# Taking GpSimd out of a second phase's weight conversions, and queueing the attention's conversions later

## The chip, the cores and the metric

One core of a Trainium2 chip runs the whole program. The metric is the device time of one execution in microseconds (us). The engines are TensorE (PE: matrix multiply; PEld: its weight loads), VectorE (DVE), ScalarE (ACT), GpSimd (POOL) and SyncE (SP), which here issues all the DMAs.

## The reference

Causal attention over 4 batches of 8 heads (576 tokens, head size 64) with a bias from a running sum, then two feed-forward blocks on 2304 tokens, all in float32:

```python
scores = scale * np.matmul(q, k.transpose(0, 1, 3, 2))
...
attn = np.exp(scores)                      # after the row maximum is taken off
attn = attn / (np.sum(attn, axis=-1, keepdims=True) + 1e-09)
x = np.matmul(attn, v)                     # -> (2304, 512)
a = x @ w1                                 # (512, 1024)
b = x @ w2
h = a * b @ w3
x2 = h @ w_out                             # (1024, 512)
h = x2 @ w_in                              # (512, 1024)
sm = softmax(h)
solu = h * sm
ln = (solu - mean) / sqrt(var + 1e-06) * g_ln
out = ln @ wo2                             # (1024, 512)
```

## The kernel before

Every large product is done as three products of split operands: a value is held as a high part (`...H`, written by a copy that rounds, `hi`) and a low part (`...L`, the value less its high part, `lo`), and PE adds high by high, high by low and low by high. The weights arrive as 64-bit floats in two 32-bit words, in jobs of 512 KB (a tile `stage` of 128 rows by 512 values), and are converted on the chip. One job is `to_f32` (a scaling of the upper words by a power of two, then three DVE instructions on lines 376, 377 and 380 that shift and join the words), then `hi` on ACT and `lo`. Two things of a job are placed on an engine by a table: the scaling (line 370 on ACT, line 372 on POOL) and the `lo` (line 97, on DVE or POOL). `ME = [(None, G), (G, V)]` deals this out in the second phase in turn: one job is scaled on ACT and its `lo` is on POOL, the next is scaled on POOL and its `lo` is on DVE. The last weight, wo2, has its own conversion, with both on POOL. A `stage` buffer is free for the next load when its `lo` has read it; there are two such buffers in the attention and four after it.

The program runs in stages that overlap a little.
- Attention, 32 heads in steps: PE makes scores (`sc`), DVE takes the maximum with line 203, ACT the exponential with line 207, DVE and ACT normalise, PE transposes (`tr`) and multiplies by v (`av`). `late` holds the `av` products of a pair of heads until the next step. Conversions of w1 and w2 (16 jobs, `wab_job`, always scaled on ACT with `lo` on DVE) are put in by `pump` in steps 3 to 17, and from step 10 the products `a` and `b` of the first block (`ab_unit`, pieces of 12 matmuls) are laid between the attention's steps as `fill`.
- The last `ab` units, with the conversions of w_out and w3 pumped between them (32 jobs with those of w_in, which `w_job` places).
- `m_unit`: the product M of w3 and w_out in 8 blocks f of 24 matmuls; each block is evicted as MH[f] by ACT and ML[f] by DVE.
- `x2_unit(c, m)`: for 256 tokens c and a column block m of 128 it adds 24 matmuls over k = 0 to 7 with MH and ML. The last k needs the last block of M. The first c has its columns done one at a time (`XMS`).
- The loop over 18 token tiles t: `h_unit` (48 matmuls in two halves of 24 and 512 columns, then the chain maximum, exponential, product, square, power on POOL, scaling with line 706), `tr2` (transposes of the result), `out_unit` (24 matmuls with wo2).

Program order alone does not set the order on an engine. A scheduler runs a model of the engines when the program is built and writes each engine's queue; `tc.issue_after(x)` holds what is issued in its scope behind x. On the chip each queue runs in order: an instruction that waits holds all that stand behind it on its engine.

Of the kernel before, what the change touches and what calls it, by code (L numbers as in the profile page):

```python
# [25 lines left out]
def tile_attention_moe(  # L26
# [15 lines left out]
    nc = tc.nc  # L42
# [38 lines left out]
    def bigtile(name):  # L81
        return PSP[0].tile([128, 2, 512], F32, tag="A", name=name)

    def smalltile(name):
        return PSP[1].tile([128, 512], F32, tag="B", name=name)
# [10 lines left out]
    def lo(dst, src, hi_, eng=nc.vector):  # L96
        eng.tensor_tensor(out=dst, in0=src, in1=hi_.bitcast(F32), op=ALU.subtract)  # L97
# [17 lines left out]
    STAT = [at.tile([128, 16], F32, name=f"STAT{i}") for i in range(PB)]  # L115

    after = [None]
    raw_t = {}
    VT = [at.tile([128, 5, 2, D], F32, name=f"VT{i}") for i in range(2)]
    XHE = None  # L120
# [71 lines left out]
    def softmax_tile(h, ti, ps_in, cut=None):  # L192
        q0, rows, n, o = QT[ti]
        pt = p_t[h]
        st = STAT[h % PB]
        dst = pt[0:rows, o:o + n]
        msk = wmask[0:rows, S - n:S] if rows == 128 else wmask[0:rows, S - 128:S - 64]
        if cut:
            dst2 = dst.rearrange("p (a b) -> p a b", a=cut)
            msk = msk.rearrange("p (a b) -> p a b", a=cut)  # L200
        else:
            dst2 = dst
        nc.vector.tensor_tensor_reduce(  # L203
            out=dst2, in0=ps_in, in1=msk, scale=-SCALE, scalar=BIG,
            op0=ALU.add, op1=ALU.min, accum_out=st[0:rows, ti:ti + 1],
        )
        nc.scalar.activation(  # L207
            out=dst, in_=dst, func=AF.Exp, bias=st[0:rows, ti:ti + 1], scale=-1.0,
            accum_out=st[0:rows, 5 + ti:6 + ti],
        )  # L210

    def qk_part(h, part):
        if part == 0:
# [34 lines left out]
    def tr_part(h, part):  # L248
        pt = p_t[h]
        PT_ = PT[h % 4]  # L250
        ps = smalltile("tr")

        def evict(dst, src):
            cnt[0] += 1
            hi(dst(PT_), src, PCOPY[cnt[0] % len(PCOPY)])

        def blk(j, q0, q1):
            o = KO[j] - 128 * j
            return lambda t: t[:, o + q0:o + q1]

        ev = []
        if part == 0:
            full = [(0, i, (i - 1) * 128) for i in range(1, 5)]
            ev = [(0, 512, blk(0, 64, S))]
        elif part == 1:
            full = [(1, i, (i - 2) * 128) for i in range(2, 5)] + [(3, 4, 384)]
            ev = [(0, 384, blk(1, 192, S)), (384, 512, blk(3, 448, S))]
        elif part == 2:
            full = [(2, i, (i - 3) * 128) for i in range(3, 5)]
            ev = [(0, 256, blk(2, 320, S))]  # L270
        else:
            full = []
        for j, i, c in full:
            nc.tensor.transpose(ps[:, c:c + 128], pt[:, QOF[i] + 128 * j:QOF[i] + 128 * j + 128], ident)  # L274
        if part == 2:
            nc.tensor.transpose(ps[0:64, 256:320], pt[0:64, QOF[0]:QOF[0] + 64], ident[0:64, 0:64])
        for c0, c1, d in ev:
            evict(d, ps[:, c0:c1])
        if part == 2:
            evict(lambda t: t[0:64, 0:64], ps[0:64, 256:320])  # L280
        if part == 3:
            for i in range(1, 5):
                nc.tensor.transpose(
                    ps[0:64, 64 * i:64 * i + 64],
                    pt[64:128, QOF[i] + 128 * i:QOF[i] + 128 * i + 64],
                    ident[64:128, 64:128],
                )
            for j in (1, 3):
                src = ps[0:64, 64 * j:64 * j + 128].rearrange("p (a b) -> p a b", a=2)
                evict(lambda t: half_view(t, j), src)  # L290
            p_t.pop(h)

    cnt = [0]
    PCOPY = [None, V]

# [94 lines left out]
        lo(dst_l, t, dst_h, e2)  # L390

    V, G = nc.vector, nc.gpsimd
    ME = [(None, G), (G, V)]
    MAT = ()
    WO2 = (0, 4, 0, 0, 0, 2, 2)
    XMS = ((0,), (1,), (2,), (3,))
    EX = 0
    AP3, AM = (2, 2, 2, 2, 2, 2, 1, 1), (3, 3, 3, 3, 3, 3, 3, 3)
    mjobs = []
# [22 lines left out]
    def pump(n):  # L422
        for _ in range(n):
            load_jobs()
            if loaded:
                raw, conv = loaded.pop(0)
                conv(raw)
        load_jobs()

    def w_job(src, dst, eng=None):  # L430
# [80 lines left out]
    for st, (h, ph) in enumerate(steps):  # L511
        for _ in range(NF.get(st, 0)):
            fill.extend(ab_unit(*units.pop(0)))
        left = len(fill)
        if st == 11:
            ps_ctx.close()
            PSP[:] = [
                ps_ctx.enter_context(tc.tile_pool(name="psE", bufs=1, space=PSUM)),
                ps_ctx.enter_context(tc.tile_pool(name="psF", bufs=6, space=PSUM)),
            ]  # L520

        def F(share):
            while fill and len(fill) > left * (1 - share):
                fill.pop(0)()

        if h is not None:
            if NQ <= h + 2 < NH:
                load_head(h + 2)
            qk_part(h, 0)
        if st > 1:  # L530
            pump(PUMP.get(st, 0))
        if h is not None:
            qk_part(h, 1)
            qk_part(h, 2)
        F(FS)
        if h is not None:
            normalise(h)
        if ph is not None:
            for part in range(4):
                tr_part(ph, part)  # L540
        if late:
            for fn in late.pop():
                fn()
        if h is not None:
            if h % 2 == 1:
                load_v(h // 2)
            if h + 1 < NH:
                split_qk(h + 1)
            if h < 2 and h + 2 < NQ:
                aug_rows(QB[h], KB[h])  # L550
            if h + 2 < NH:
                if h + 2 < NQ:
                    load_head(h + 2)
                load_aug(h + 2, cumf_scr[h + 2:h + 3] if h + 2 < NQ else cum_scr[h + 2])
        F(1)
        if ph is not None and ph % 2:
            parts = av_parts(ph // 2)
            if ph < PD or st == len(steps) - 1:
                for fn in parts:
                    fn()  # L560
            else:
                late.append(parts)
    attn_ctx.close()


    NT = T // 128
# [85 lines left out]
    def x2_unit(c, *ms):  # L652
# [2 lines left out]
            x2_t[c] = [r2.tile([128, KC, 256], F32R, tag=f"x2{i}", bufs=2, name=f"x2{i}") for i in "hl"]  # L655
        XH, XL = x2_t[c]
        GH, GL = g_hl[c]
        ps = {m: smalltile("x2")[:, 0:256] for m in ms}
        for k0, k1 in ((0, KF - 1), (KF - 1, KF)):
            for m in ms:  # L660
                for k in range(k0, k1):
# [103 lines left out]
            raws[k] = stage(wo2[k * 128:k * 128 + 128])  # L765

    def wo2_conv(k):
        t = to_f32(raws.pop(k), G)
        nc.scalar.activation(out=t, in_=t, func=AF.Copy, scale=gln[:, k:k + 1])
        hi(OH[:, k], t)  # L770
        lo(OL[:, k], t, OH[:, k], nc.gpsimd)
        wo2_load(k + 4)

    nwo = [0]
# [1 line left out]
    def wo2_pump(c):  # L776
        for _ in range(c):
            wo2_conv(nwo[0])
            nwo[0] += 1
# [13 lines left out]
    for t in range(NT + 2):  # L793
# [7 lines left out]
        if t < NT and c + 1 < NCH and 2 * t + 1 >= EX:  # L801
            x2_unit(c + 1, 2 * o + 1)
        if t < 2:
            wo2_pump(WO2[5 + t])
        if 0 <= t - 2 < NT:
            out_unit(t - 2)
        if t == NT:
# [55 lines left out]
```

## Time and profile before

| | us |
|---|---|
| three runs | 787.57, 788.91, 792.77 |
| median | 788.91 |
| profiled execution | 790.51 |
| its span, first to last instruction | 788.70 |
| PE busy | 756.8 (96%) |
| DVE busy | 472.9 (60%) |
| ACT busy | 396.5 (50%) |
| POOL busy | 157.7 (20%) |

The profiled execution has 1.81 us outside its span and is 1.60 us above the median. A busy share is a mean over stages. Matmul ends are modelled, so the pitch of a row of matmuls (its time by its count) says more than their busy time. "PEclk" is the granted clock of TensorE as a share of its full 2.4 GHz; 0.50 is its lower level, 1.2 GHz.

### The profile page before, as it was taken

The numbers are of one execution on the slowest core, as the hardware profiler recorded it, in microseconds if no ns is written. First come the engines' busy times: TensorE is split into PE (matmuls) and PEld (weight loads), VectorE is DVE, ScalarE is ACT, GpSimd is POOL, SyncE is SP. The second block draws the span as 40 slices with busy tenths as digits, with TensorE's granted clock in tenths as the row PEclk, the third lists the DMA queues.
The fourth block names the chain that finished last, engine by engine and source line by source line (L and its number), as shares of the span: only waits on it lengthen the run. The fifth ranks groups of instructions, "written<-read, shape, count | busy, mean of one in ns | idle before, by whom it ended". The sixth has DMA issues, their size and how long they took to land.

```text
span 788.7 us, 13075 instructions
## 1 busy us (share of the span) xinstructions
PE 756.8 (96%) x4864; PEld 658.4 (83%) x4864; DVE 472.9 (60%) x1162; ACT 396.5 (50%) x927; POOL 157.7 (20%) x165
## 2 busy tenths in 40 slices
PE   8988998999999999999899979899999999999997
PEld 5556888988888898999888868788888888888886
DVE  5898889787656564328867998744424343432241
ACT  4986787698666665414325345633323243322232
POOL 6022313234222211003412546300000000000000
PEclk9998999999999999999999979999999999999999
DMA  5643454334333320016649455102022000000001
GB/s 138 197 115 102 144 172 142 104 98 131 107 92 90 94 77 31 31 63 227 209 140 345 170 183 165 54 14 68 14 67 63 31 14 14 14 15 14 14 27 40
DMA packets 38039, 75.59 MB, mean 96 GB/s; under 512 B 6796, under 2 KB 18060, under 8 KB 37976
## 3 DMA queue, kind: packets, MB, share of 16 engines
q1 hardware_dynamic: 37976, 74.76, 30.9%
q8 instruction: 38, 0.62, 0.3%
q14 instruction: 25, 0.20, 0.1%
HBM read 60.36 MB, written 14.38 MB: 95 GB/s over the span
## 4 chain that ended last, share of the span: by engine, by line
PE 75%; DVE 6%; DMA 3%; POOL 2%; issue 2%; ACT 2%; SPq 0%; ACTq 0%; DVEq 0%; POOLq 0%
PE o L732 13%; PE a L334 12%; PE b L334 11%; PE h L683 11%; PE x L663 11%; PE av L306 4%; PE tr L274 3%; PE sc L189 3%; PE sc L190 2%; PE m L589 2%; PE tr L721 2%; DMA stage<-in_w_dram 2%; DVE stage L377 1%; DVE stage L376 1%; DVE stage L380 1%
## 5 line engine op out<-in xcount | busy, mean ns | idle before, releaser
L207 ACT ACTIVATE P<-P,STAT 128x448 f32<-128x448 f32 (+4 forms) x160 | 87.9, 551 | 30.0 <-DVE STAT L203 28.6
L691 DVE TENSOR_REDUCE sv<-h 128x1 f32<-128x1024 f32 x18 | 22.0, 1223 | 114.3 <-PE h L683 114.3
L663 PE MATMUL x<-gh,MH 128*128 128x256 f32 x288 | 84.0, 292 | 3.1 <-ACT MH L92 3.1
L663 PE MATMUL x<-gh,ML 128*128 128x256 f32 x288 | 82.6, 287 | 2.2 <-DVE ML L97 2.2
L663 PE MATMUL x<-gl,MH 128*128 128x256 f32 x288 | 82.6, 287 | 0.0
L97 POOL TENSOR_TENSOR QA<-qk,QB 64x576 fp32r<-64x576 f32 x24 | 34.6, 1441 | 208.9 <-ACT QB L92 170.1
L203 DVE CUSTOM_DVE_ANT_0 P<-sc,wmask 128x448 f32<-128x448 f32 (+4 forms) x160 | 70.2, 478 | 9.5 <-PE sc L181 6.5
L705 POOL TENSOR_TENSOR sv<-sv,mhalf 128x1 f32<-128x1 f32 x18 | 10.0, 555 | 261.7 <-DVE sv L702 261.7
L334 PE MATMUL a<-xT0h,W 128*128 128x288 f32 x256 | 59.1, 305 | 2.5 <-ACT a_sb L346 1.8
L663 PEld LDWEIGHTS x<-gh,MH 128*128 128x128 f32 x288 | 56.4, 196 | 4.4 <-ACT MH L92 3.6
L334 PE MATMUL b<-xT1h,W 128*128 128x288 f32 x256 | 57.0, 297 | 2.9 <-DVE g_sb L354 2.8
L663 PEld LDWEIGHTS x<-gh,ML 128*128 128x128 f32 x288 | 56.4, 196 | 2.5 <-DVE ML L97 2.4
L334 PE MATMUL b<-xT0h,W 128*128 128x288 f32 x256 | 58.2, 302 | 0.2 <-DVE g_sb L354 0.2
L334 PE MATMUL a<-xT1h,W 128*128 128x288 f32 x256 | 57.2, 298 | 0.5 <-ACT a_sb L346 0.5
L732 PE MATMUL o<-OH,lh 128*128 128x512 f32 x144 | 57.2, 397 | 0.3 <-ACT lh L92 0.3
L683 PE MATMUL h<-IH,x2l 128*128 128x512 f32 x144 | 56.7, 394 | 0.8 <-DVE x2l L97 0.8
L732 PE MATMUL o<-OH,ll 128*128 128x512 f32 x144 | 57.1, 396 | 0.0
L663 PEld LDWEIGHTS x<-gl,MH 128*128 128x128 f32 x288 | 56.4, 196 | 0.8
L732 PE MATMUL o<-OL,lh 128*128 128x512 f32 x144 | 56.9, 395 | 0.0
L683 PE MATMUL h<-IL,x2h 128*128 128x512 f32 x144 | 56.5, 392 | 0.0
L683 PE MATMUL h<-IH,x2h 128*128 128x512 f32 x144 | 56.2, 390 | 0.0
L693 ACT ACTIVATE e<-h,sv 128x1024 f32<-128x1024 f32 x18 | 20.1, 1115 | 66.7 <-DVE sv L691 66.7
(125 smaller groups left out, 1995.5 us busy)
## 6 DMA issues: line engine op xcount, KB each, us to landing
stage<-in_w_dram SPq DMA_DIRECT2D x32, 512.0 KB
qk<-in_qk_dram SPq DMA_DIRECT2D x48, 288.0 KB
g_scr<-g_sb SPq DMA_DIRECT2D x32, 288.0 KB
stage<-in_wo_dram SPq DMA_DIRECT2D x16, 512.0 KB
graw<-g_scr SPq DMA_DIRECT2D x6, 1024.0 KB
out_dram<-o SPq DMA_DIRECT2D x18, 256.0 KB
VT<-in_vm_dram SPq DMA_DIRECT2D x16, 256.0 KB
stage<-in_w_in_dram SPq DMA_DIRECT2D x8, 512.0 KB
```

Of the source, the lines that this page charges most:

```text
L97: eng.tensor_tensor(out=dst, in0=src, in1=hi_.bitcast(F32), op=ALU.subtract)
L189: nc.tensor.matmul(view, QB[h % 2][:, q0:q0 + rows], KB[h % 2][:, c0:c0 + w], start=True, stop=False)
L203: nc.vector.tensor_tensor_reduce(out=dst2, in0=ps_in, in1=msk, scale=-SCALE, scalar=BIG, op0=ALU.add, op1=ALU.min, accum_out=st[0:rows, ti ...
L207: nc.scalar.activation(out=dst, in_=dst, func=AF.Exp, bias=st[0:rows, ti:ti + 1], scale=-1.0, accum_out=st[0:rows, 5 + ti:6 + ti],)
L274: nc.tensor.transpose(ps[:, c:c + 128], pt[:, QOF[i] + 128 * j:QOF[i] + 128 * j + 128], ident)
L306: nc.tensor.matmul(st["ps"][64 * e:64 * e + 64, 448 + c0:448 + c1], vr[:, j, e], PT[(2 * p + e) % 4][:, o + c0:o + c1], **kw,)
L334: nc.tensor.matmul(ps, w_[:, c, fs], x_[:, c, sl], start=(c == 0 and w_ is WH and x_ is XH), stop=(c == KC - 1 and w_ is WL),)
L663: nc.tensor.matmul(ps[m], w_[:, k, m * 128:m * 128 + 128], g_[:, k], start=(k == 0 and w_ is MH and g_ is GH), stop=(k == KF - 1 and w_ is ...
L683: nc.tensor.matmul(ps[:, hf], x_[:, k, ts_], w_[:, k, hf * 512:hf * 512 + 512], start=(k == 0 and x_ is XH and w_ is IH), stop=(k == KC - ...
L691: nc.vector.reduce_max(out=sv[:, 0:1], in_=psf, axis=AX.X, negate=True)
L693: nc.scalar.activation(out=e, in_=psf, func=AF.Exp, bias=sv[:, 0:1], scale=1.0, accum_out=sv[:, 1:2])
L732: nc.tensor.matmul(ps, l_[:, k], w_[:, k], start=(k == 0 and l_ is LH and w_ is OH), stop=(k == KF - 1 and l_ is LL),)
```

## The change

In the second phase every conversion has its scaling on ACT and its `lo` on DVE (`ME` has one entry), and so has wo2. The first `x2_unit` takes all four columns in one call: first k = 0 to 6 of all four, then the last k of each; two of the four sums lie in a large PSUM tile that otherwise holds `h`. The conversions of wo2 that stood in the loop over t at entries 5 and 6 of `WO2` are at 2 and 3, with the same counts. In the attention, a pumped conversion is held behind the first maximum and the first exponential of its step (`behind`, set in `softmax_tile`), and the held `av` products behind the last transposition (`last_tr`).

```diff
-        nc.vector.tensor_tensor_reduce(
+        mx = nc.vector.tensor_tensor_reduce(
...
-        nc.scalar.activation(
+        ex = nc.scalar.activation(
...
+        if ti == 0:
+            behind[:] = [mx.ins, ex.ins]
...
-                nc.tensor.transpose(
+                last_tr[0] = nc.tensor.transpose(
...
-    ME = [(None, G), (G, V)]
+    ME = [(None, V)]
...
-    WO2 = (0, 4, 0, 0, 0, 2, 2)
-    XMS = ((0,), (1,), (2,), (3,))
+    WO2 = (0, 4, 2, 2)
+    XMS = ((0, 1, 2, 3),)
...
                 raw, conv = loaded.pop(0)
-                conv(raw)
+
+                with ExitStack() as order:
+                    for ins in behind:
+                        order.enter_context(tc.issue_after(ins))
+                    conv(raw)
...
-            for fn in late.pop():
-                fn()
+            with tc.issue_after(last_tr[0].ins):
+                for fn in late.pop():
+                    fn()
...
-        ps = {m: smalltile("x2")[:, 0:256] for m in ms}
+        if len(ms) == KC:
+            two = bigtile("x2")
+            ps = {m: smalltile("x2")[:, 0:256] if m < 2 else two[:, m - 2, 0:256] for m in ms}
+        else:
+            ps = {m: smalltile("x2")[:, 0:256] for m in ms}
...
-        t = to_f32(raws.pop(k), G)
+        t = to_f32(raws.pop(k), None)
...
-        lo(OL[:, k], t, OH[:, k], nc.gpsimd)
+        lo(OL[:, k], t, OH[:, k])
```

Each line after the first of these edits stands four or more lines lower in the changed kernel (line 203 becomes 204, 370 becomes 374, 376, 377 and 380 become 380, 381 and 384).

The first place is ACT's queue in the attention, in the softmax of head 7 (`STAT_102`), before the change:

```order
L240 ACTIVATE P<-P,STAT_101 128x448
L92 ACTIVATE W_105<-stage 128x4x128
L207 ACTIVATE P,STAT_102<-P,STAT_102 128x448
L370 ACTIVATE stage<-stage 128x512
L207 ACTIVATE P,STAT_102<-P,STAT_102 64x64
L92 ACTIVATE KA<-qk_606 128x576
```

and the same place in the changed kernel:

```order
L243 ACTIVATE P<-P,STAT_101 128x448
L92 ACTIVATE PT_95<-tr 64x2x64
L208 ACTIVATE P,STAT_102<-P,STAT_102 128x448
L208 ACTIVATE P,STAT_102<-P,STAT_102 64x64
L92 ACTIVATE KA<-qk_606 128x576
```

The scaling of a job (line 370) stood between two exponentials of the head and is gone from there: ACT's next one now follows the first exponential of head 8.

The second place is ACT's queue at the evictions of M's last two blocks (`MH<-m`), with the conversions of w_in (`IH`), before:

```order
L370 ACTIVATE stage<-stage 128x512
L92 ACTIVATE IH<-stage 128x512 x3
L92 ACTIVATE MH<-m 128x512
L370 ACTIVATE stage<-stage 128x512
L92 ACTIVATE IH<-stage 128x512
L370 ACTIVATE stage<-stage 128x512
L92 ACTIVATE IH<-stage 128x512
L92 ACTIVATE MH<-m 128x512
```

and after:

```order
L92 ACTIVATE IH<-stage 128x512
L92 ACTIVATE MH<-m 128x512
L92 ACTIVATE IH<-stage 128x512
L374 ACTIVATE stage<-stage 128x512 x2
L92 ACTIVATE IH<-stage 128x512
L92 ACTIVATE MH<-m 128x512
```

Five high parts of w_in stand ahead of the last MH before, four after; two scalings stand between the last two MH both times.

The third place is PE's queue in the attention at the first `b` piece of block f = 4 (weights `W_111` high and `W_112` low), before, where the piece runs through:

```order
L334 MATMUL b<-xT0h,W_111 128x288
L334 MATMUL b<-xT0l,W_111 128x288
L334 MATMUL b<-xT0h,W_112 128x288
L334 MATMUL b<-xT0h,W_111 128x288
L334 MATMUL b<-xT0l,W_111 128x288
```

and after, where scores of two heads stand ahead of it and a third set, of another head, behind its second matmul:

```order
L190 MATMUL sc<-KB_89,QB_87 128x288
L191 MATMUL sc<-KA,QA 128x288
L338 MATMUL b<-xT0h,W_111 128x288
L338 MATMUL b<-xT0l,W_111 128x288
L190 MATMUL sc<-KB_90,QB_88 128x448
L191 MATMUL sc<-KA,QA 128x448
L190 MATMUL sc<-KB_90,QB_88 64x64
L191 MATMUL sc<-KA,QA 64x64
```

The third matmul of the piece, the first that reads the low part, has moved behind those scores, a whole `a` piece, two more matmuls of the next `b` piece and three transpositions.

## Rows read from the trace of the kernel before

**Rows 1.** Windows by stage: span us, then each engine's busy us, PE's clock, DMA, GB/s.

```profile
16.00:140.00 124.00, 111.67 (x710) 88.38 (x710) 106.81 (x313) 98.21 (x257) 27.31 (x16) 0.94 0.51 151
140.00:355.00 215.00, 215.00 (x1689) 193.45 (x1689) 122.88 (x407) 136.36 (x367) 46.64 (x32) 1.00 0.29 82
355.00:408.90 53.90, 49.94 (x365) 48.32 (x363) 44.96 (x73) 19.71 (x38) 17.43 (x15) 1.00 0.60 198
408.90:452.57 43.67, 43.65 (x192) 36.16 (x193) 33.15 (x50) 18.65 (x32) 15.83 (x12) 1.00 0.72 239
452.57:514.00 61.43, 52.61 (x331) 48.33 (x330) 53.90 (x89) 31.77 (x58) 28.23 (x23) 0.89 0.41 135
```

**Rows 2.** Timeline of PE, 450 to 500: start, us, and in brackets the wait ahead.

```profile
457.45 0.58 PE L663 MATMUL x<-gh,ML 128*128 128x256 f32 x1 [2.15 <-DVE ML L97]
...
462.23 0.58 PE L663 MATMUL x<-gh,MH 128*128 128x256 f32 x1 [3.13 <-ACT MH L92]
...
472.97 0.40 PE L683 MATMUL h<-IH,x2h 128*128 128x512 f32 x1
...
478.45 0.50 PE L683 MATMUL h<-IH,x2l 128*128 128x512 f32 x1 [0.80 <-DVE x2l L97]
...
497.29 1.09 PE L721 MATMUL tr<-ident,so 128*128 128x128 f32 x8 [2.74 <-DVE so L706]
```

**Rows 3.** Windows behind the longest of these waits, columns as in rows 1.

```profile
457.40:467.50 10.10, 6.92 (x30) 6.63 (x31) 8.89 (x14) 3.35 (x7) 4.90 (x5) 0.50 0.54 176
...
497.20:502.00 4.80, 4.71 (x28) 4.71 (x29) 4.09 (x9) 3.60 (x7) 1.51 (x2) 0.64 0.01 3
```

**Rows 4.** Chain of waits, 511 to 526: start, us, what.

```profile
511.06 2.82 PE x L663 x24
...
519.47 5.49 PE h L683 x24
```

**Rows 5.** Groups of instructions, 355 to 500: busy us, mean ns, idle before.

```profile
L377 DVE SCALAR_TENSOR_TENSOR stage<-stage 128x512 uint32<-128x512 uint32 x40 | 33.8, 847 | 3.6 <-POOL stage L372 2.9 <-ACT stage L370 0.3
L380 DVE SCALAR_TENSOR_TENSOR stage<-stage 128x512 uint32<-128x512 uint32 x40 | 32.7, 820 | 0.2
L376 DVE TENSOR_SCALAR stage<-stage 128x512 uint32<-128x512 uint32 x40 | 23.7, 591 | 8.2 <-DMA stage<-in_wo_dram 4.1 <-DMA stage<-in_w_dram 3.4 <-DMA stage<-in_w_in_dram 0.7
L372 POOL TENSOR_SCALAR stage<-stage 128x512 f32<-128x512 f32 x24 | 21.7, 902 | 100.9 <-ACT a_sb L346 59.7 <-DMA stage<-in_w_dram 21.9 <-DMA stage<-in_wo_dram 4.4
L97 POOL TENSOR_TENSOR w3l<-stage,w3h 128x512 fp32r<-128x512 f32 x8 | 14.1, 1768 | 19.0 <-ACT w3h L92 19.0
...
L370 ACT ACTIVATE stage<-stage 128x512 f32<-128x512 f32 x16 | 11.0, 689 | 23.9 <-DMA stage<-in_w_in_dram 9.0 <-DMA stage<-in_wo_dram 8.2 <-DMA stage<-in_w_dram 6.7
...
L97 DVE TENSOR_TENSOR w3l<-stage,w3h 128x512 fp32r<-128x512 f32 x8 | 5.5, 685 | 4.4 <-ACT w3h L92 4.4
```

**Rows 6.** Instructions on the tile stage, 355 to 500: shortest, median, longest ns.

```profile
L376 DVE TENSOR_SCALAR stage<-stage x40: 414/422/1547, 356.5 to 493.9; 128x512 uint32<-128x512 uint32 x40
L377 DVE SCALAR_TENSOR_TENSOR stage<-stage x40: 673/681/1807, 357.3 to 494.9; 128x512 uint32<-128x512 uint32 x40
L380 DVE SCALAR_TENSOR_TENSOR stage<-stage x40: 672/682/1726, 358.0 to 498.3; 128x512 uint32<-128x512 uint32 x40
```

**Rows 7.** Chain of waits, 452 to 482, columns as in rows 4.

```profile
454.33 1.58 POOL IL L97
...
455.93 4.43 DMA stage<-in_w_in_dram
```

**Rows 8.** Timeline of PE, the longest of four waits between 384 and 398.

```profile
384.23 0.40 PE L334 MATMUL b<-xT1h,W 128*128 128x288 f32 x1 [1.56 <-DVE g_sb L354]
```

**Rows 9.** Timelines of PE and ACT and a window in the attention, 55 to 70.

```profile
60.22 0.41 PE L283 MATMUL tr<-ident,P 64*64 64x64 f32 x4 [1.44 <-DVE STAT L203]
...
57.54 0.67 ACT L370 ACTIVATE stage<-stage 128x512 f32<-128x512 f32 x1 [2.12 <-DMA stage<-in_w_dram]
...
60.00:70.00 10.00, 8.51 (x42) 5.17 (x42) 7.31 (x20) 5.17 (x14) 0.74 (x1) 0.66 0.54 166
```

More of the change, by code (lines that the diff above doesn't have):

```diff
@@ L117, in tile_attention_moe @@
     after = [None]
+    behind = []
     raw_t = {}
@@ L291, in tr_part @@
             p_t.pop(h)
+    last_tr = [None]
     cnt = [0]
@@ L563, in tile_attention_moe @@
     attn_ctx.close()
+    behind.clear()
     NT = T // 128
@@ L803, in tile_attention_moe @@
         if t < 2:
-            wo2_pump(WO2[5 + t])
+            wo2_pump(WO2[2 + t])
         if 0 <= t - 2 < NT:
```

## The prediction

> **What bounds the kernel now.** I first read the windows by stage, to see where PE is not the limit. Between 140 and 355 us PE is busy for all of the 215.00 us and the granted clock is 1.00 [rows 1]; nothing can be won there. The loop over token tiles behind 514 us is the same: its blocks of 24 matmuls take 2.82 and 5.49 us in an unbroken chain of PE [rows 4], and the order of its instructions is not touched. What is left lies in four places [rows 1]: the attention's first 124 us (12.3 us idle, clock 0.94, so 124 × 0.06 = 7.4 us lost to the lower level of 1.2 GHz), the tail of the `ab` units from 355 to 408.9 (4.0 us idle, clock 1.00), the blocks of M from 408.9 to 452.57 (no idle time) and the first `x2` and `h` from 452.57 to 514 (8.8 us idle, clock 0.89, 6.8 us lost).
>
> PE's timeline then says for what it waits in the last of these: 2.15 us for an ML at 457.45, 3.13 us for an MH at 462.23, 0.80 us for the low part of x2 and 2.74 us for `so` of the first token tile [rows 2]. After these pauses the granted clock is 0.50 for 10.1 us and 0.64 for 4.8 us [rows 3], so a pause costs its length and a slow stretch behind it. The attention has the same picture in small: a wait of 1.44 us at 60.22 (and one like it of 1.27 us at 62.49) and a clock of 0.66 over 60 to 70, which alone is 3.4 us [rows 9].
>
> Last I read the groups of DVE and POOL in the second phase, because the waits of M's blocks and of the tail lead to DVE. From 355 to 514 DVE is busy for 45.0 + 33.2 + 53.9 = 132 of 159 us [rows 1], so it has 27 us left. Its three shift-and-join instructions last much longer on average than in the median: 591 against 422, 847 against 681, 820 against 682 ns, with longest ones of 1547 to 1807 ns [rows 5, 6]. At 40 of each that is 6.8 + 6.6 + 5.5 = 18.9 us above the median.
>
> **The change part by part.** *POOL's share goes to ACT and DVE.* 24 scalings leave POOL (902 ns each) and cost ACT 24 × 0.689 = 16.5 us; 24 `lo` leave POOL (1768 ns each for w3) and cost DVE 24 × 0.685 = 16.4 us [rows 5]. The long instances lie where POOL works, with the `lo` on POOL itself 1.58 us long [rows 7], so with POOL quiet I expect the three DVE instructions at their medians. DVE then pays 16.4 and gets back up to 18.9 us: as a load it is between −2.5 (all of the excess gone) and +16.4 us (none), and I take about zero, since medians so close to the shortest (422 to 414, 681 to 673, 682 to 672) leave little else that could stretch the longest. The Trainium skill, "SBUF — State Buffer", section "Who interferes with whom", says that DVE and GpSimd share one pair of ports as an exclusive lock, which whoever starts first holds for its whole instruction, and that a DVE instruction with two SBUF inputs collides with GpSimd's reads; the longest of 1547 against a median of 422 agrees, and by that rule the whole 18.9 goes. ACT is busy for 45% of its time in these three windows (70.1 of 159 us) [rows 1], and 16.5 us more are covered by its idle time; the cover ends where its waits grow, which is the second rival.
>
> *The first x2.* From 452.57 to the first `h` at 472.97 the first `x2` takes 20.4 us [rows 2], where four columns at 2.82 us [rows 4] are 11.3; so 9.1 us are lost, 5.3 in the two waits [rows 2] and the rest at half clock [rows 3]. With all columns at once, 4 × 21 = 84 matmuls of 0.1175 us (2.82 by 24) stand ahead of the first that needs block 7: 9.9 us instead of 2.5. Even if MH7 comes as late as before, at about 462.2, it is then needed only at 462.4, so the 3.13 us go. The 2.15 us for ML of block 6 remain at worst: its matmul stands as early as before, and only an earlier DVE helps. The second place in the order helps a little (four instead of five high parts of w_in ahead of MH7). So the ends are −3.1 (ML6 as late as before, the half clock behind it kept) and −9.1; I take −8, because DVE on its medians should reach ML6 at least 2 us sooner: with the excess falling at 18.9 by 40 jobs, 0.47 us a job, the ten or so jobs of the M stage alone give 4.7 us, and take back about five `lo` of 0.685 = 3.4, and the tail before has done the same.
>
> *h and the norm of the first tile.* The 0.80 us for x2l should nearly stay, as two evictions at the end of four columns come in a row; the fourth column's last trio sits behind an eviction of its tile-mate. The 2.74 us for `so` and the 1.7 us of slow clock behind it (4.8 × 0.36) [rows 2, 3] stay too: line 706 of the first tile stands behind the second tile's maximum in the queue. Taken together 0, with ends of −5.2 (all of it gone) and +3 (an eviction more per pair, and a slow stretch of the length shown). wo2's conversions lie in the loop, in DVE's and ACT's idle time.
>
> *The tail.* Four waits sum to 3.2 us, the longest 1.56 us on DVE behind a queue of conversions [rows 8]. A DVE without long instances removes most: −2. The ends are −3.2 and +4: every scaling now waits on ACT for its load, and an `a_sb` eviction stands behind it.
>
> *The attention.* In the first place of the order the scaling between two exponentials of head 7 goes; it waited 2.12 us for its load there at 57.54 and held ACT's queue, and PE's two waits at 60.22 and 62.49 come right behind it [rows 9]. Gone with the slow clock, that is 1.44 + 1.27 + 3.4 = 6.1 us; since part of the slow stretch began before these waits, I take −4. Moved past are ACT's and DVE's instructions of the step and, with the release of the buffer, the next load on SP's queue. The price stands in the third place: the low part of f = 4 comes so late that its `b` piece is split, and W arrives in one burst between heads 8 and 16. DVE has some 10 us of work between the two low parts there against 6.2 us of PE's, so a wait of up to 3.8 us could appear; for the three blocks f = 4 to 6 I take +1. Together −3, ends −9 (the other two pauses of this stage vanish as well) and +6 (two such waits, less the gain).
>
> The sum: 790.5 − 8 + 0 − 2 − 3 = 777.5 us against the profiled execution, 1.81 us outside the span unchanged. That execution is 1.6 us above the median of the three runs, so 775.9, **776 us** for the median.
>
> **The rivals.** *DVE takes the place of the shared lock.* If the long instances don't come from POOL, DVE gains the 24 `lo` and loses nothing. 16 of them (8 of w_in, 8 of wo2) come behind 408.9: 11 us on an engine that is idle for 10.5 + 7.5 us there [rows 1]. ML6 and ML7 come later, x2 wins nothing, the tail neither; 790.5 − 3 − 1.6 = **786 us**. For it speaks DVE's 88% in the last window; against it the gap of mean and median in rows 6. The Trainium skill, "Perfetto Trace Analysis", section "Optimizing Scalar/DVE Operations", says that a saturated DVE may be relieved by Scalar or even GpSimd, which speaks against this change, but adds that between DVE and GpSimd it may not help.
>
> *ACT's queue becomes the bound (the slower side).* 16 scalings waited 23.9 us for loads on ACT, 1.49 us each [rows 5]; each wait holds MH, `a_sb` and high parts behind it. With 40 scalings at that wait ACT is taken for 70.1 + 16.5 + 59.8 = 146 of 159 us. It decides from 1.8 us a scaling ((159 − 86.6) / 40). A load takes 4.43 us from its buffer's release [rows 7], and the one in the attention waited 2.12 us [rows 9]: at that, ACT needs 86.6 + 84.8 = 171 us, 12 more than the stretch has, and the gains of x2 and tail are gone: 790.5 − 3 + 12 − 1.6 = **798 us**. For it speaks that POOL waited out loads for scalings till now (26.3 us); against it that POOL's slow scaling and `lo` were part of the ring that releases buffers, and that is now shorter.
>
> *More than forecast.* All pauses of the attention go (−9), ML6 is in time (−9.1), the `so` wait goes in part: 790.5 − 9 − 9.1 − 2 − 4 − 1.6 = **765 us**.
>
> *It doesn't do what it says.* The scheduler could have kept the old order; the queues show that it did not, so this has next to no chance (789 us).
>
> **How the numbers follow.** The forecast with its neighbourhood (769 to 782) has 0.60, the DVE rival 0.20, the ACT rival 0.10, the larger gain 0.08, no effect 0.02. The range reaches from 766 to 788: it takes in the DVE rival and most of the larger gain, and leaves the ACT rival out. One per cent, 7.9 us, is about what a measurement of this kernel tells from no change; so faster by more than that is below 781: nearly all of the forecast and the larger gain, 0.66. Within 1%: the DVE rival, no effect and a little of the forecast, 0.24. Slower: 0.10.
>
> **What the profile after would show.** Right: DVE's three instructions with a mean within 5% of 422, 681 and 682 ns; the first `x2` within 13 us and no clock of 0.50 behind it; no wait for MH before it; the wait for `so` still there; in the attention a clock near 1.00 over 60 to 70. Wrong: waits on ML or g_sb of 2 us or more with DVE busy throughout (first rival); scalings on ACT with over 1.8 us of wait each for their loads and PE waiting for MH or `a_sb` (second); PE's waits for W between heads 10 and 16 of over 3 us with half clock behind them. The forecast fails most easily if M's blocks wait for conversions where they did not before, since that stretch has no idle time to absorb it.

## The result and the profile after

The changed kernel takes 779.8 us in the median of 4 runs (778.5 to 781.4), against 788.7 for the kernel before; the ratio is 0.987 (95% interval 0.985 to 0.990). It was forecast at 776 with a range of 766 to 788. The gain of 9 us is there, but two of its terms (the tail, and `h` behind the first x2) were not of the size that the forecast gave them, and for one part of the change, the order of the first x2, no run shows a share in it.

The profiled execution has a span of 777.7 us, 11.0 less than before. The medians are only 8.9 apart, so some 2 us of the differences by stage below are scatter between single executions. Four marks cut the span into stages: the end of the attention's last but one group of 24 `av` (its start in PE's timeline plus its duration; the last group ends 19.0 us later in every kernel here), the first matmul of M, the first of x2 and the end of the span.

| | last but one av group ends | first m | first x2 | end |
|---|---|---|---|---|
| before | 333.3 | 408.9 | 452.6 | 788.7 |
| after | 330.2 | 400.9 | 444.6 | 777.7 |
| stage: before, after | 333.3, 330.2 | 75.6, 70.7 | 43.7, 43.7 | 336.1, 333.1 |
| difference | −3.1 | −4.9 | 0.0 | −3.0 |

The groups of instructions of the changed kernel from 345 to 500 answer to [rows 5]:

```profile
L374 ACT ACTIVATE stage<-stage 128x512 f32<-128x512 f32 x40 | 27.9, 696 | 31.3 <-DMA stage<-in_w_dram 12.2 <-DMA stage<-in_wo_dram 9.5 <-DMA stage<-in_w_in_dram 9.3
L381 DVE SCALAR_TENSOR_TENSOR stage<-stage 128x512 uint32<-128x512 uint32 x40 | 27.4, 686 | 0.3 <-ACT stage L374 0.3
L384 DVE SCALAR_TENSOR_TENSOR stage<-stage 128x512 uint32<-128x512 uint32 x40 | 27.3, 685 | 0.0
...
L380 DVE TENSOR_SCALAR stage<-stage 128x512 uint32<-128x512 uint32 x40 | 17.0, 426 | 12.0 <-DMA stage<-in_wo_dram 5.5 <-DMA stage<-in_w_dram 4.5 <-DMA stage<-in_w_in_dram 1.8
```

The means of DVE's three, 426, 686 and 685 ns, are now within 1% of the medians of before. Their sum went from 90.2 us [rows 5] to 71.7, so 18.5 of the 18.9 us above the median are gone. DVE took over 16.4 us of `lo` without getting fuller: its busy time over the whole span is 466.0 us against 472.9. ACT makes all 40 scalings and waits 31.3 us for their loads, 0.78 us each, half of the 1.49 of before.

PE's timeline, its waits from 400 to 490 (columns as in [rows 2]):

```profile
400.92 0.50 PE L599 MATMUL m<-WOH,w3h 128*128 128x512 f32 x1 [0.62 <-DVE g_sb L358]
...
459.62 0.50 PE L697 MATMUL h<-IH,x2h 128*128 128x512 f32 x1 [1.92 <-ACT x2h L92]
...
480.62 0.47 PE L697 MATMUL h<-IH,x2h 128*128 128x512 f32 x1 [1.50 <-DVE so L711]
...
484.19 0.50 PE L697 MATMUL h<-IH,x2l 128*128 128x512 f32 x1 [1.49 <-DVE x2l L97]
...
487.08 1.46 PE L735 MATMUL tr<-ident,so 128*128 128x128 f32 x8 [2.39 <-DVE so L720]
```

The four waits of the tail [rows 8] are gone, and so are those for ML and MH in the first x2 [rows 2]. In their place stand 1.92 us for the high part of x2, 1.50 for a `so`, and 1.49 for a low part; the wait of the first transposition for `so` is 2.39 us (2.74 before). The windows of the changed kernel for the first x2 (to the first `h`) and the stretch behind it, with its first 3.5 us; then for the place of [rows 9] and the next pause of the attention:

```profile
444.59:459.62 15.03, 13.12 (x112) 12.91 (x110) 13.42 (x26) 8.23 (x15) 0.00 (x0) 1.00 0.55 179
459.62:487.08 27.46, 22.07 (x114) 18.81 (x114) 24.72 (x50) 20.27 (x37) 0.56 (x1) 0.94 0.48 151
460.00:463.50 3.50, 3.50 (x17) 3.36 (x16) 3.45 (x9) 2.18 (x4) 0.00 (x0) 0.55 0.76 253
...
60.00:70.00 10.00, 10.00 (x73) 7.15 (x72) 6.64 (x25) 6.48 (x15) 1.47 (x2) 1.00 0.36 92
105.00:127.00 22.00, 17.05 (x115) 15.11 (x115) 18.30 (x50) 14.99 (x34) 3.28 (x2) 0.90 0.50 146
```

The stretch from the first x2 matmul to the first `h` has no slow clock any more and is 15.0 us long instead of 20.4. The two lengths are not of the same work: 96 x2 matmuls stand in it before, 111 after. The 15 more belong to the next block of tokens and are worth 1.8 us at 0.1175 each. Behind the wait of 1.92 us the clock is 0.55 for 3.5 us. In the attention the stretch from 60 to 70 went from 8.51 us of PE work at 0.66 to 10.00 at 1.00; in exchange PE is idle for 5.0 of the 22 us from 105 (1.1 before), as its timeline says:

```profile
121.76 0.37 PE L190 MATMUL sc<-KB,QB 128*128 128x288 f32 x1 [3.82 <-issue]
123.66 0.61 PE L338 MATMUL b<-xT0h,W 128*128 128x288 f32 x1 [1.13 <-ACT W L92]
```

### The profile page after: what moved, and what is told of

Same layout as the page of the kernel before. It is cut to its first block, busy times and chain, and to the rows that moved or that the text cites. A ratio compares the mean times of both kernels' runs of the same rounds, so it can differ in the third digit from the quotient of the medians.

```text
span 777.7 us, 13025 instructions
## 1 busy us (share of the span) xinstructions
PE 749.4 (96%) x4864; PEld 653.1 (84%) x4864; DVE 466.0 (60%) x1186; ACT 412.9 (53%) x951; POOL 97.3 (13%) x117
## 4 chain that ended last, share of the span: by engine, by line
PE 80%; DVE 8%; DMA 7%; issue 2%; ACT 1%; POOL 1%; SPq 0%; DVEq 0%; ACTq 0%; POOLq 0%
PE o L746 13%; PE a L338 12%; PE b L338 12%; PE h L697 11%; PE x L677 11%; PE av L310 5%; PE tr L277 4%; PE sc L182 3%; PE sc L190 2%; PE sc L191 2%; PE tr L735 2%; DMA stage<-in_w_dram 2%; DMA stage<-in_w_in_dram 2%; DMA graw<-g_scr 1%; DVE stage L381 1%
## 5 line engine op out<-in xcount | busy, mean ns | idle before, releaser
L208 ACT ACTIVATE P<-P,STAT 64x64 f32<-64x64 f32 (+4 forms) x160 | 88.0, 551 | 32.0 <-DVE STAT L204 29.4
L204 DVE CUSTOM_DVE_ANT_0 P<-sc,wmask 64x64 f32<-64x64 f32 (+4 forms) x160 | 70.9, 481 | 13.0 <-PE sc L182 8.7
L374 ACT ACTIVATE stage<-stage 128x512 f32<-128x512 f32 x56 | 38.3, 689 | 32.5 <-DMA stage<-in_w_dram 13.3
```

The costliest lines, as they stand in the source:

```text
L204: mx = nc.vector.tensor_tensor_reduce(out=dst2, in0=ps_in, in1=msk, scale=-SCALE, scalar=BIG, op0=ALU.add, op1=ALU.min, accum_out=st[0:row ...
L208: ex = nc.scalar.activation(out=dst, in_=dst, func=AF.Exp, bias=st[0:rows, ti:ti + 1], scale=-1.0, accum_out=st[0:rows, 5 + ti:6 + ti],)
L374: nc.scalar.activation(out=high.bitcast(F32), in_=high.bitcast(F32), func=AF.Copy, scale=2.0 ** -112)
```

## The experiments

All times are medians, each with the ratio to the kernel before that was measured beside it. "Stages" are the end of the last but one `av` group, the stretch from there to M, and from x2 to the end, by the marks above; M itself took 43.7 to 43.9 us in all of them. Stages come from one profiled execution each. That of e2 took 784.1 us and that of e1 788.5, 4 and 3 us above their medians; the changed kernel and its repetition (e13) differ by 1.4 us at the first mark.

| | us | ratio, 95% interval | stages |
|---|---|---|---|
| before | 787.6 to 788.8 | | 333.3, 75.6, 336.1 |
| changed | 779.8 | 0.987 (0.985 to 0.990) | 330.2, 70.7, 333.1 |
| e1_att_only | 785.5 | 0.997 (0.994 to 1.001) | 331.5, 74.6, 336.5 |
| e2_engines_only | 780.1 | 0.990 (0.987 to 0.993) | 334.8, 70.7, 333.1 |
| e3_x2_only | 792.7 | 1.007 (1.003 to 1.010) | 334.3, 74.5, 339.4 |
| e4_wo2_pool | 781.4 | 0.993 (0.989 to 0.996) | 331.2, 70.7, 333.9 |
| e5_scale_pool | 782.8 | 0.992 (0.990 to 0.995) | 331.5, 72.2, 334.0 |
| e6_lo_pool | 779.4 | 0.989 (0.985 to 0.993) | 330.5, 70.7, 333.3 |
| e7_late_only | 783.6 | 0.994 (0.992 to 0.996) | 335.9, 70.7, 333.2 |
| e9_no_x2_order | 777.5 | 0.987 (0.983 to 0.991) | 332.0, 70.7, 331.0 |
| e10_pool_beside | 788.1 | 1.001 (0.999 to 1.003) | 330.5, 74.5, 336.9 |
| e11_gln_fold | 779.0 | 0.989 (0.986 to 0.992) | 328.6, 70.7, 333.7 |
| e12_fold_no_x2 | 777.3 | 0.985 (0.982 to 0.989) | 331.2, 70.7, 330.3 |
| e13_changed_again | 780.1 | 0.989 (0.986 to 0.992) | 331.6, 70.8, 332.6 |

**Each part alone.** The three kernels keep one part of the change and undo the others; the edits here and below are against the changed kernel. The attention's part alone:

```diff
-    ME = [(None, V)]
+    ME = [(None, G), (G, V)]
-    WO2 = (0, 4, 2, 2)
-    XMS = ((0, 1, 2, 3),)
+    WO2 = (0, 4, 0, 0, 0, 2, 2)
+    XMS = ((0,), (1,), (2,), (3,))
...
-        t = to_f32(raws.pop(k), None)
+        t = to_f32(raws.pop(k), G)
...
-        lo(OL[:, k], t, OH[:, k])
+        lo(OL[:, k], t, OH[:, k], nc.gpsimd)
...
-            wo2_pump(WO2[2 + t])
+            wo2_pump(WO2[5 + t])
```

> Only the attention's part on the kernel before (conversions behind the first maximum, v behind the last transposition). If the parts add up as the stages of the two traces do, this is worth the 2.8 to 3.1 us by which the last av of the attention ends earlier: about 785.7 against 788.7. Rival: the 3 us were won only because the later stage drew fewer things forward, or the burst of W eats the gain when the tail is as slow as before: 788 to 790.

It came to 785.5, by its median a gain of 2.2 us, but the interval includes no change. Its first mark is at 331.5, and its later stages are within 1.1 us of those of before.

The engines' part alone:

```diff
-    WO2 = (0, 4, 2, 2)
-    XMS = ((0, 1, 2, 3),)
+    WO2 = (0, 4, 0, 0, 0, 2, 2)
+    XMS = ((0,), (1,), (2,), (3,))
...
-                    for ins in behind:
+                    for ins in ():
...
-            with tc.issue_after(last_tr[0].ins):
+            with ExitStack():
...
-            wo2_pump(WO2[2 + t])
+            wo2_pump(WO2[5 + t])
```

> Only the engines' part on the kernel before: second-phase scalings on ACT, lo on DVE, wo2 too; first x2 still one column at a time. If POOL's work was what stretched DVE, the three DVE instructions go to means of about 426, 686 and 685 ns, the tail gains its 4.9 us, and ML of block 6 comes 2 us earlier, so that the first x2 loses only the wait for block 7: about 780 to 783. Rival, DVE as the new bound: the instructions stay stretched or the added lo eat it, 787 to 790.

It came to 780.1, at the lower end of what was expected, and its profile has both stage gains of the changed kernel, 75.6 to 70.7 and 336.1 to 333.1. The first x2 takes 12.9 us here, for 96 matmuls, with a wait for MH of 1.33 us in place of 3.13. So most of the 9.1 us that it had lost go without its new order. Behind the first `h` a wait of 4.17 us for a high part of x2 appears that the kernel before doesn't have.

The order of the first x2 alone:

```diff
-    ME = [(None, V)]
+    ME = [(None, G), (G, V)]
...
-                    for ins in behind:
+                    for ins in ():
...
-            with tc.issue_after(last_tr[0].ins):
+            with ExitStack():
...
-        t = to_f32(raws.pop(k), None)
+        t = to_f32(raws.pop(k), G)
...
-        lo(OL[:, k], t, OH[:, k])
+        lo(OL[:, k], t, OH[:, k], nc.gpsimd)
```

> Only the order of the first x2 (all columns, then the last block) on the kernel before, POOL still converting. If the order alone hides the wait for block 7, the 3.13 us go, but the 2.15 us for ML of block 6 and the slow clock behind it stay: 784 to 787. Rival: the gain of x2 is the engines' alone (blocks 6 and 7 earlier): 788 or more, since the evictions of four columns now come in a row.

It is slower than before, 792.7, ratio above 1 with its whole interval. The wait for the last block of M is gone as meant, but a longer one came behind it. PE's timeline of this kernel, the last matmul of the first x2 and the first `h`:

```profile
469.04 0.28 PE L677 MATMUL x<-gh,ML 128*128 128x256 f32 x1
475.15 0.79 PE L697 MATMUL h<-IH,x2h 128*128 128x512 f32 x1 [5.83 <-ACT x2h L92]
```

and ACT's in the same time:

```profile
469.28 0.67 ACT L92 ACTIVATE IH<-stage 128x512 fp32r<-128x512 f32 x1 [3.29 <-DVE stage L384]
472.12 0.77 ACT L783 ACTIVATE stage<-stage,gln 128x512 f32<-128x512 f32 x1 [2.18 <-DVE stage L384]
472.93 0.69 ACT L92 ACTIVATE OH<-stage 128x512 fp32r<-128x512 f32 x1
474.07 0.77 ACT L783 ACTIVATE stage<-stage,gln 128x512 f32<-128x512 f32 x1 [0.46 <-DVE stage L384]
474.74 0.63 ACT L92 ACTIVATE x2h<-x 128x256 fp32r<-128x256 f32 x2
```

PE is done with the columns at 469.3, and their evictions (`x2h<-x`) stand in ACT's queue behind a high part of w_in and three instructions of two conversions of wo2, which wait for DVE's last join (line 384). One column at a time, the evictions lie between the columns, and the kernel before has no wait ahead of its first `h` [rows 2].

"The order" here takes in one more thing. The first four conversions of wo2 are put in behind the first call of `x2_unit`: that is behind the first column before, and behind all four in the changed kernel. The runs with and without the order differ in both, and the two were not separated.

The three parts alone win 2.2, 7.5 and −5.0 us, together 4.7, and the whole change 8.9: they don't add up, since the order costs less where the engines' part is there.

**What POOL does to DVE.** This kernel adds to the changed one 24 subtractions on POOL whose result nobody reads; in the traces the instructions of PE, ACT and DVE are those of the changed kernel, in the same order. POOL has nothing else to do between 345 and 450, so the added work delays no other work of POOL.

```diff
+    side, nj = [], [0]
...
         lo(dst_l, t, dst_h, e2)
+        if side and nj[0] < 24:
+            nj[0] += 1
+            f = dst_h.rearrange("p a b -> p (a b)") if len(dst_h.shape) == 3 else dst_h
+            lo(ML[:, 7], f.bitcast(F32), f, nc.gpsimd)
...
+    side.append(ML)
```

> The changed kernel with 24 added subtractions on POOL that nobody reads, one behind the high part of each job of w_out and w3, written over a block of ML before that is computed; the queues of PE, DVE, ACT and SP are those of the changed kernel. If a subtraction on POOL stretches DVE's instructions beside it, the means of DVE's three go up again by some 24 x 1 us over the stretch of these jobs, to 550, 800 and 800 ns or so, and the tail is 2 to 4 us longer: 782 to 785. Rival, the long instances came from something else in the queues of before: means stay at 426, 686 and 685 ns and the time at 779.8.

They take back the gain: 788.1, 8.3 us above the changed kernel's 779.8 and not different from before by the interval. The stretch to M is 74.5 us again, and the one behind x2 336.9. The added instructions and DVE's three, in the groups from 345 to 500:

```profile
L384 DVE SCALAR_TENSOR_TENSOR stage<-stage 128x512 uint32<-128x512 uint32 x40 | 30.2, 759 | 0.0
L381 DVE SCALAR_TENSOR_TENSOR stage<-stage 128x512 uint32<-128x512 uint32 x40 | 29.1, 727 | 0.3 <-ACT stage L374 0.3
L97 POOL TENSOR_TENSOR ML<-w3h 128x512 fp32r<-128x512 f32 x16 | 24.0, 1501 | 38.8 <-ACT w3h L92 38.1 <-POOL ML L97 0.4
L380 DVE TENSOR_SCALAR stage<-stage 128x512 uint32<-128x512 uint32 x40 | 23.6, 593 | 6.5 <-DMA stage<-in_wo_dram 4.2 <-DMA stage<-in_w_dram 1.6 <-DMA stage<-in_w_in_dram 0.6
```

and three of the meetings in its timelines, POOL first, then DVE:

```profile
386.28 1.04 POOL L97 TENSOR_TENSOR ML<-w3h 128x512 fp32r<-128x512 f32 x1 [2.97 <-ACT w3h L92]
389.06 1.25 POOL L97 TENSOR_TENSOR ML<-w3h 128x512 fp32r<-128x512 f32 x1 [1.74 <-ACT w3h L92]
392.66 1.04 POOL L97 TENSOR_TENSOR ML<-w3h 128x512 fp32r<-128x512 f32 x1 [2.35 <-ACT w3h L92]
```

```profile
386.49 1.12 DVE L380 TENSOR_SCALAR stage<-stage 128x512 uint32<-128x512 uint32 x1
...
389.70 0.90 DVE L380 TENSOR_SCALAR stage<-stage 128x512 uint32<-128x512 uint32 x1
...
393.02 1.23 DVE L384 SCALAR_TENSOR_TENSOR stage<-stage 128x512 uint32<-128x512 uint32 x1
```

The shift of 0.42 us that starts at 386.49, in the middle of POOL's subtraction (386.28 to 387.32), ends at 387.61, 0.29 us behind it; the next, against POOL's end at 390.31, ends at 390.60, again 0.29 behind; and the join of 0.68 us ends 0.55 behind POOL's end at 393.70. The rows read as if DVE stood until POOL's instruction is over and then did most of its own. It is so throughout: of the lengthened DVE instructions between 345 and 450, the 13 that overlap just one single POOL instruction end 0.27 to 0.29 us (shifts) or 0.54 to 0.55 us (two inputs) behind it. ACT's scalings are not lengthened (686 ns in the mean, 696 in the changed kernel). The Trainium skill, "SBUF — State Buffer", section "Who interferes with whom", describes an exclusive lock on a shared pair of ports that the first to issue holds for its whole instruction, for `tensor_scalar` in its 2-port modes, and says that a DVE instruction with two SBUF inputs contends with GpSimd's reads; these meetings agree with it.

Two kernels give POOL a real share again, the one the `lo` of every second job, the other the scaling:

```diff
-    ME = [(None, V)]
+    ME = [(None, V), (None, G)]
```

> The changed kernel with every second lo of w_out, w3 and w_in back on POOL, scalings all on ACT. If the lo on POOL (two inputs) is what collides with DVE, DVE's three instructions have means near 550, 780 and 760 ns as in the kernel before and the time is 783 to 786. Rival, DVE's relief of 16 lo counts for more than the collisions: 777 to 779.

```diff
-    ME = [(None, V)]
+    ME = [(None, V), (G, V)]
```

> The changed kernel with every second scaling of w_out, w3 and w_in back on POOL, every lo on DVE: 16 scalings leave ACT. If scalings on POOL stretch DVE too, and DVE gets no lo off its hands, this is the worst of both: means of DVE's three near 480 to 550, 720 to 780 and 720 to 780 ns and 783 to 787 us. Rival, only the lo with its two inputs collides: means at 426, 686 and 685 ns and 778 to 781.

DVE's three in the groups of the kernel with `lo` on POOL:

```profile
L384 DVE SCALAR_TENSOR_TENSOR stage<-stage 128x512 uint32<-128x512 uint32 x40 | 29.5, 740 | 0.3
L381 DVE SCALAR_TENSOR_TENSOR stage<-stage 128x512 uint32<-128x512 uint32 x40 | 29.1, 729 | 0.5 <-ACT stage L374 0.3
L380 DVE TENSOR_SCALAR stage<-stage 128x512 uint32<-128x512 uint32 x40 | 22.1, 554 | 10.0 <-DMA stage<-in_wo_dram 3.7 <-DMA stage<-in_w_in_dram 3.4 <-DMA stage<-in_w_dram 2.4
```

and of the one with scalings:

```profile
L384 DVE SCALAR_TENSOR_TENSOR stage<-stage 128x512 uint32<-128x512 uint32 x40 | 29.4, 740 | 0.1
L381 DVE SCALAR_TENSOR_TENSOR stage<-stage 128x512 uint32<-128x512 uint32 x40 | 28.1, 704 | 0.9 <-POOL stage L376 0.5 <-ACT stage L374 0.3
L380 DVE TENSOR_SCALAR stage<-stage 128x512 uint32<-128x512 uint32 x40 | 17.8, 446 | 11.8 <-DMA stage<-in_wo_dram 4.7 <-DMA stage<-in_w_dram 4.5 <-DMA stage<-in_w_in_dram 2.3
```

With every second `lo` on POOL the collisions return, 29.5 + 29.1 + 22.1 against 71.7 us, 9.0 more, but DVE is rid of 16 × 0.685 = 11.0 us, and the time is 779.4, no different from the changed kernel's. The expectation that the collisions alone would count was wrong. With scalings on POOL the collisions are 3.6 us and DVE is rid of nothing: 782.8, 2.8 above the 780.1 that the changed kernel took beside it (e13), and the stretch to M is 72.2. Here it is ACT that is relieved, and that brought nothing. The remaining piece, wo2 on POOL:

```diff
-        t = to_f32(raws.pop(k), None)
+        t = to_f32(raws.pop(k), G)
...
-        lo(OL[:, k], t, OH[:, k])
+        lo(OL[:, k], t, OH[:, k], nc.gpsimd)
```

> The changed kernel with wo2's eight scalings and lo back on POOL. In the changed kernel the stretch from the first h to the first out product is about 2 us longer than before, with waits for x2h, x2l and so. If the 8 jobs that wo2 puts on ACT and DVE there cause it, this kernel is 1 to 3 us faster than the changed one (777 to 779) and its so wait shrinks. If POOL's contention comes back instead (DVE's instructions beside it stretched to 1.5 us), it is 1 to 4 us slower (781 to 784).

781.4 against 779.8 is on the side of the collisions, but the intervals overlap, and the stretch behind x2 (333.9) tells no difference from 333.1. That wo2's load on ACT and DVE is what lengthens the stretch behind the first `h` is not confirmed. The test is a partial one: wo2's second scaling (by `g_ln`) and its high part stay on ACT, its joins on DVE.

**The order of the first x2 under the engines' part.** The changed kernel with its columns one at a time again:

```diff
-    WO2 = (0, 4, 2, 2)
-    XMS = ((0, 1, 2, 3),)
+    WO2 = (0, 4, 0, 0, 0, 2, 2)
+    XMS = ((0,), (1,), (2,), (3,))
...
-            wo2_pump(WO2[2 + t])
+            wo2_pump(WO2[5 + t])
```

> The changed kernel with the first x2 again one column at a time (attention's and engines' parts kept). The engines' part alone gave a first x2 of 12.9 us, the changed kernel has 15.0, and the stretch from x2 to the end is 333.1 us in both. If the order of x2 gives nothing once the engines' part is there, this kernel is within 1 us of the changed one (779 to 781). Rival, the order of x2 gives its share as forecast: 784 or more. A third case, the order costs time: 776 to 778.

777.5: the gain is all there without the order. Its first x2 takes 12.4 us (446.34 to 458.77) for 96 matmuls, against 15.0 for 111. Behind the first `h` it has this wait on PE's timeline, of a kind that e2 (4.17 us) and e12 (3.27) share:

```profile
484.51 0.80 PE L697 MATMUL h<-IH,x2h 128*128 128x512 f32 x1 [4.09 <-ACT x2h L92]
```

While PE waits, ACT runs three instructions of wo2's conversions (0.76, 0.67 and 0.70 us) and an exponential (1.12 us), and then the high part. Whether the order costs something was tried once more, with wo2's scaling by `g_ln` folded in, with the order of the changed kernel and without:

```diff
-        nc.scalar.activation(out=t, in_=t, func=AF.Copy, scale=gln[:, k:k + 1])
-        hi(OH[:, k], t)
-        lo(OL[:, k], t, OH[:, k])
+        nc.scalar.activation(out=OH[:, k], in_=t, func=AF.Copy, scale=gln[:, k:k + 1])
+        nc.vector.scalar_tensor_tensor(
+            out=OL[:, k], in0=t, scalar=gln[:, k:k + 1], in1=OH[:, k].bitcast(F32), op0=ALU.mult, op1=ALU.subtract,
+        )
```

> The changed kernel with wo2's second scaling (by g_ln) folded into its high part on ACT and into its lo on DVE: eight ACT instructions of about 0.77 us go, DVE's lo becomes a product and a subtraction of the same size. If ACT's queue is what makes the x2h and so waits behind the first h, 1 to 3 us are won (777 to 779). If DVE's queue sets these waits, no change: 779 to 781.

> The changed kernel with the first x2 one column at a time and wo2's scaling by g_ln folded into high part and lo. If both alterations (2.4 and 0.8 us by their medians) are real and add up, 776 to 777, ratio to the kernel before near 0.985. If they were scatter, 779 to 780.

> The changed kernel itself, beside the others of this call: 779 to 780, ratio 0.987. It is the measure for whether the kernel with the old order of x2 is faster than it by more than scatter.

The fold is worth nothing that these runs show (779.0 against 779.8 to 780.1; 777.3 against 777.5). Without the order the two medians are 777.3 and 777.5, with it 779.0 to 780.1 in three; but the intervals overlap, and of the profiles without it two have 330.3 and 331.0 us from x2 to the end and one (e2) 333.1, where those with it have 332.6 to 333.7. Two kernels that don't hold the conversions point the same way: e2, without the order, took 780.1, and e7, with it, 783.6 (e7 also holds `av`). So no run shows a gain by the order; that it costs 2 us is likely, not shown. The fastest version by its median is the one without it and with the fold.

**The two holds in the attention.** The changed kernel without the hold of the conversions:

```diff
-                    for ins in behind:
+                    for ins in ():
```

> The changed kernel without the hold of the attention's conversions (the av products still held behind the last transposition). If the attention's 2.8 us come from the conversions' place, they go: 782 to 783. If they come from the place of the av products, 779 to 780. Rival, without the burst of W behind head 10 it is faster: 777 or less.

783.6 against 780.1 of the changed kernel beside it (e13). Its first mark is at 335.9, where the ten kernels with both holds lie between 328.6 and 332.0 (330.9 in the mean) and the three with neither (before, e2, e3) between 333.3 and 334.8. The attention's gain needs the hold of the conversions. The hold of `av` was not run without the other's company, so what it does for them stays open.

## Why the prediction was right, and where its terms were not

*DVE's load.* Right as argued: mean above median meant collisions with POOL, and they went when POOL was quiet (18.5 us). The kernel with idle subtractions (e10) shows the cause: POOL's added work is all that differs in it. The first rival (DVE as the new bound) fell with the means; it returns as a matter of balance only, where each `lo` kept on DVE costs about as much as its collisions (e6).

*The first x2.* Taken as −8. It won all of the 9.1 us that were lost in it: the changed kernel's x2 matmuls up to the first `h` run without a wait and at clock 1.00. That MH7 would come "as late as before" was wrong, and so was the share of the order. In the changed kernel its eviction ends 4.1 us after the first x2 matmul (448.16 + 0.58 against 444.59); before it ended 9.6 us after (461.60 + 0.57 against 452.57). With that only 1.0 to 1.3 us were left for the order to hide (the waits for MH in e9, e12 and e2), not 3.13. Most of the term is the engines' part: without the order the 96 matmuls take 12.4 to 12.9 us, 7.5 to 8.0 less than before.

*h and the norm of the first tile.* This is the step that failed: "taken together 0", with +3 as its end. x2 to the end won 3.0 us, and with 9.1 of them from x2 itself this term came to about +6. The first `out` matmul tells the same: it comes 57.8 us after the first of x2 where it came 61.2 after, with the same matmuls ahead of it, which makes +5.7. Of this, 1.92 us are the wait for x2h ahead of the first `h`, 1.9 are more idle time behind it (5.4 against 3.5), and 1.8 more time lost to the slow clock there (42.7 us at 0.92 against 40.8 at 0.96). The forecast saw the evictions in a row but not what they stand behind on ACT. In the changed kernel two high parts of w_in, which wait for DVE's joins, and two scalings come ahead of them. The end of that row, on ACT's timeline:

```profile
457.47 0.67 ACT L92 ACTIVATE IH<-stage 128x512 fp32r<-128x512 f32 x1 [0.26 <-DVE stage L384]
458.62 0.68 ACT L374 ACTIVATE stage<-stage 128x512 f32<-128x512 f32 x1 [0.48 <-DMA stage<-in_wo_dram]
459.20 0.93 ACT L92 ACTIVATE x2h<-x 128x256 fp32r<-128x256 f32 x3
```

The order is not the whole of it. By the same sum the term is +2.0 to +4.5 in e12, e9 and e2, which do without the order. What makes that part stays open; the forecast's "in DVE's and ACT's idle time" for wo2 is the suspect, which e4 did not confirm.

*The tail.* Taken as −2 with −3.2 as its end, measured −4.9. The mechanism was right, the size was read from too few rows. The waits went (4.0 us of idle time to M before, 0.6 after), and PE's busy time in the stretch fell by 1.6 us too, for the same matmuls (71.7 to 70.1 us), of which the list of waits tells nothing. All kernels with the engines' part and no scalings or idle work on POOL in the tail have 70.7 or 70.8 us here.

*The attention.* Taken as −3, measured −3.1 between the two profiled executions and 3.5 by removing the hold. Its composition was not as forecast. The stretch from 60 to 70 is won, and waits for W in the burst behind head 10 appeared (1.13 and one of 1.07 us). But the idle time from 16 to 140 did not shrink: 12.3 us before, 13.0 after. What shrank is the slow clock, 0.94 to 0.96, about 2.5 us of 124. The pause of 3.82 us at 121.76 is not the wait for W that was priced at up to 3.8 us; that the figures agree is luck. The scores behind it start 0.11 us after DVE has read the scores before them (line 204), and that maximum stands in DVE's queue behind two shifts and a join of held conversions:

```profile
115.48 2.01 DVE L380 TENSOR_SCALAR stage<-stage 128x512 uint32<-128x512 uint32 x2
...
120.91 0.74 DVE L204 CUSTOM_DVE_ANT_0 P<-sc,wmask 128x576 f32<-128x576 f32 x1
```

The two shifts take 2.01 us beside a subtraction on POOL (115.47 to 117.20). The pause is 3.81 or 3.82 us in all ten kernels with both holds and is missing in the four others (before, e2, e3, e7), so it comes with the hold of the conversions. That it is a wait for this maximum is read from the times; the profile names no releaser.

*ACT's queue, the slower rival.* It needed more than 1.8 us of wait per scaling; there were 0.78. Before, ACT and POOL together waited 23.9 + 26.3 = 50.2 us for the loads of their 40 scalings, after it is 31.3. That fits the argument against this rival, that POOL's slow instructions leave the ring of buffers; no run tests it alone.

The sum was −13 and came out as −11 between the profiled executions: x2 −9.1 in place of −8, `h` +6.1 in place of 0, the tail −4.9 in place of −2, the attention −3.1 in place of −3. That the total came so near is in part luck, since an error of 6 in one term was offset by 4 in two others.

## What to carry to other kernels

Where the mean of a DVE instruction lies well above its median, look at what POOL does in the long ones: moving POOL's work onto DVE itself can be free, if the collisions it ends are as long as the work it adds (16.4 us taken over, 18.5 given back here), and a POOL that is given work nobody needs can cost as much as a whole optimisation gained. Before hiding a wait by reordering, ask whether another part of the same change already brings the awaited data earlier, and what the evictions that now come in a row stand behind.

## What had not been expected of the hardware

That 24 instructions of 1.4 to 1.5 us in the mean on POOL (35.0 us of its busy time), with no reader and the same order of work on PE, ACT and DVE, cost 8.3 us of kernel time. And that the scaling on POOL, with a single input, also stretches DVE: the joins of lines 381 and 384 by 18 and 55 ns on the mean of 40, with 16 scalings.
